# Attention before a routed expert layer: where the loads of q, k and v are asked for

## The chip, the cores and the metric

The kernel runs on one core of one Trainium2 chip. The metric is device time in microseconds (us) of one execution. The core has a matrix engine (PE, with its weight loads shown as PEld), a vector engine (DVE), a scalar engine (ACT), a general engine (POOL) and a sync engine (SP) that here does little but issue DMAs.

## The reference

Attention over 8 batches of 8 heads, 576 tokens of 64 channels, with a causal mask and a bias that decays with a running sum of `s`; then each token goes through one of eight two-layer experts, chosen by a gate that may keep the expert of the token before.

```python
scores = scale * np.matmul(q, k.transpose(0, 1, 3, 2))
bias = -(cum[:, :, :, None] - cum[:, :, None, :])
scores = np.where(causal, -1000000000.0, scores + np.minimum(bias, 0.0))
attn = np.exp(scores - np.max(scores, axis=-1, keepdims=True))
attn = attn / (np.sum(attn, axis=-1, keepdims=True) + 1e-09)
x = np.matmul(attn, v)            # heads side by side: 512 channels a token
...
h = np.maximum(x[b, s] @ w1[e], 0.0)
out[b, s] = p[e] * (h @ w2[e])
```

## The kernel before, in words

Two heads of a batch make one unit `n`; there are 32 of them (`NPAIR`). The attention part is a loop over 16 **slots** `m`; slot `m` works on the units `2m` and `2m+1`. All instructions are written in program order, one stream for each engine, and an engine takes its stream strictly in that order. In one slot PE does this:

1. **The stretch of scores** (`scores`, line 1125): six groups of matmuls, three for each of the two units, 40 matmuls in all. ACT takes the exponential of each group (line 1126), POOL masks it.
2. In some slots a router product (`lp`, line 230, in slots 4, 8, 12; `pos`, line 315, in slots 6, 10, 14).
3. **The stretch of values**: first the diagonal blocks of this slot's first unit (`values_halves`, line 1196), then the diagonal scores of the *next* slot's two units (`scores_halves(m + 1)`, line 1147, tile `ph`: 16 matmuls for unit `2m+2`, then 16 for unit `2m+3`), then line 1196 for the second unit, then 84 small matmuls into `po` and 84 into `pb` (`values`, line 1184). DVE divides and moves the results out (`evacuate`, line 1206), and later scales the v tiles of units to come (`weigh`, line 1102).

A unit needs three loads from DRAM: `kb` and `qb` (288 KB each, line 1273) and `va` (320 KB, line 1026). There are four buffers for `kb`, four for `qb` and six for `va`. The units 0 to 3 are loaded ahead of the loop; slot `m` asks for later units, six loads a slot, all on SP's queue. `transfers(m)` says at which place in the slot each load is asked for. A place is the end of one instruction: `e{u}{i}` is the exponential of group `u` of the slot's unit `i` (so `e00`, `e10`, `e20`, `e01`, `e11`, `e21` in the order of time, all belonging to the stretch of scores); `h` comes with the last exponential, but stands behind the diagonal scores in program order; `x0`, `x1` are the two reciprocals of the first unit's evacuation, `y0`, `y1` those of the second. SP waits for that instruction, then issues the DMA; SP's own stream is in program order too.

Other DMAs on SP in this part: `wx` (line 207, after slot 1's loads), `ends` and `wend` (lines 1090, 1092) and four stores of `table<-pad` (line 202) between the loads of slots 2 and 3; quarters of the first expert's weights (line 572) at `y1` of slots 11 to 14; fetches of rows from the table (line 582) in slot 14. POOL issues indirect stores into the table (line 363) in slots 6 to 15.

The scores of unit `n` are read in slot `n // 2`, but its diagonal scores one slot earlier:

```python
halves = banks("ph") if b + 1 < NPAIR else None
to = room(b)
scores_halves(m + 1, halves)
values_halves(b, to, True)
let_go("h", exps[b, 2])
```

Of the kernel before, what the change touches and what calls it, by code (L numbers as in the profile page):

```python
# [23 lines left out]
NPAIR = B * HP  # L24
# [97 lines left out]
def held(tc, dma, behind):  # L122

    if behind is not None:
        tc.add_manual_dep(dma.ins, behind.name, mybir.DependencyInfo(mybir.DependencyClass.Sync, mybir.DependencyReason.DATA),
                          reason="a transfer's time")
# [860 lines left out]
def attention(ctx, tc, q, k, v, s, wx, ident, recs, wend, router, experts):  # L987
# [32 lines left out]
    def load_v(n, behind=None):  # L1020

        if n >= NPAIR:
            return
        b, hp = divmod(n, HP)
        va = vs[n] = p_v.tile([P, NB, 2, DH], F32, name="va")
        held(tc, nc.sync.dma_start(va.rearrange("p c h d -> p (c h d)"), v[b, hp].rearrange("p c h d -> p (c h d)")), behind)
# [207 lines left out]
    for g in range(NG - 1):  # L1234
        m = HP * GB // 2 * (g + 1)
# [9 lines left out]
        for c in range(NC):  # L1245
# [3 lines left out]
            i, p = places[c]  # L1249
# [3 lines left out]
    m = NPAIR // 2  # L1253
# [14 lines left out]
    def qk_part(n, what):  # L1268
        def load(behind):
            b, hp = divmod(n, HP)  # L1270
            to = p_in.tile([P, S], F32, name=what + "b")
            ins.setdefault(n, [None, None])["qk".index(what)] = to
            held(tc, nc.sync.dma_start(to, (q, k)["qk".index(what)][b][:, hp]), behind)
        return load

    def v_part(n):
        return lambda behind: load_v(n, behind)

    def transfers(m):

        n = 2 * m + NV
        k0, q0, k1, q1 = (qk_part(n + i, x) for i in range(2) for x in "kq")
        if m == 0:
            return {"e11": v_part(4), "h": k0, "x0": q0, "x1": k1, "y0": q1}
        if m == 1:
            return {"e00": v_part(5), "e10": v_part(6), "e20": k0, "e11": q0, "h": k1, "x0": q1, "x1": v_part(7)}
        of = {"e00": v_part(n), "e20": v_part(n + 1), "e11": k0, "h": q0, "x0": k1, "x1": q1} if n < NPAIR else {}
        i = m - NPAIR // 2 + 5
        if 0 <= i < 4:
            of["y1"] = lambda behind: experts.load(0, 0, i, behind)  # L1290
        return of
# [7 lines left out]
    for m in range(NPAIR // 2):  # L1299
        pair = 2 * m, 2 * m + 1  # L1300
        waiting = transfers(m)
        for n in pair:
            for u in range(len(UNITS)):
# [623 lines left out]
```

## Time and profile before

| | |
|---|---|
| median of three runs | 695.86 us (693.32, 695.86, 697.61) |
| profiled execution, its own time | 695.28 us |
| its span, first to last instruction | 693.4 us |
| mean granted TensorE clock | 0.998 |
| PE busy | 674.5 us, 97% of the span |
| DVE, POOL, ACT busy | 525.5, 385.9, 199.9 us |
| moved by DMA | 158.18 MB, mean 228 GB/s |

The span runs from the first to the last instruction; the execution's own time has 1.88 us around it. The attention loop takes the first 205 us or so, the expert layer the rest. Times of rows are from the start of the span.

### The profile page before, as it was taken

The numbers are of one execution on the slowest core, as the hardware profiler recorded it, in microseconds if no ns is written. First come the engines' busy times: TensorE is split into PE (matmuls) and PEld (weight loads), VectorE is DVE, ScalarE is ACT, GpSimd is POOL, SyncE is SP. The second block draws the span as 40 slices with busy tenths as digits, with TensorE's granted clock in tenths as the row PEclk, the third lists the DMA queues.
The fourth block names the chain that finished last, engine by engine and source line by source line (L and its number), as shares of the span: only waits on it lengthen the run. The fifth ranks groups of instructions, "written<-read, shape, count | busy, mean of one in ns | idle before, by whom it ended". The sixth has DMA issues, their size and how long they took to land.

```text
span 693.4 us, 19173 instructions
## 1 busy us (share of the span) xinstructions
PE 674.5 (97%) x7837; PEld 586.2 (85%) x7837; DVE 525.5 (76%) x978; ACT 199.9 (29%) x368; POOL 385.9 (56%) x547
## 2 busy tenths in 40 slices
PE   8999989989999999999999999999999999999995
PEld 7787877878888889999998999999687997779984
DVE  4564857877975797989989997787568686779762
ACT  5454635536432112122221221212121122112121
POOL 3462366867776768746446367555433473525642
PEclk9999999999999999999999999999999999999999
DMA  8565565767659888499848447264988979866001
GB/s 259 186 207 157 158 199 154 229 202 229 204 158 406 254 274 300 152 335 350 302 187 302 156 169 287 88 257 140 349 289 336 394 282 317 270 251 257 31 13 39
DMA packets 54968, 158.18 MB, mean 228 GB/s; under 512 B 11156, under 2 KB 31636, under 8 KB 49111
## 3 DMA queue, kind: packets, MB, share of 16 engines
q1 hardware_dynamic: 47751, 136.52, 58.6%
q0 software_dynamic: 6880, 20.10, 7.6%
q8 instruction: 64, 1.05, 0.6%
q14 instruction: 33, 0.27, 0.1%
q10 hardware_dynamic: 240, 0.25, 0.1%
HBM read 136.21 MB, written 20.85 MB: 227 GB/s over the span
## 4 chain that ended last, share of the span: by engine, by line
PE 89%; DVE 3%; issue 3%; DMA 2%; POOL 1%; ACT 1%; POOLq 0%; ACTq 0%; DVEq 0%
PE p L687 27%; PE p L691 26%; PE ps L1125 11%; PE po L1184 6%; PE pb L1184 6%; PE hp L781 4%; PE hp L772 2%; PE yp L804 2%; DMA w1b<-in_w_dram 2%; PE lp L230 1%; PE ph L1147 1%; PE po L1196 1%; DVE wt L617 1%; DMA qb<-in_q_dram 1%; PE pb L1196 1%
## 5 line engine op out<-in xcount | busy, mean ns | idle before, releaser
L691 PE MATMUL p<-w2b,hT 128*128 128x256 f32 (+1 forms) x720 | 164.9, 380 | 1.9 <-DVE w2b L617 1.1
L691 PEld LDWEIGHTS p<-w2b,hT 128*128 128x128 f32 (+1 forms) x720 | 132.8, 187 | 24.6 <-issue 3.1
L687 PE MATMUL p<-xT,w1b 128*128 128x128 f32 (+1 forms) x1280 | 151.2, 275 | 1.4 <-DVE w1b L617 0.9
L687 PEld LDWEIGHTS p<-xT,w1b 128*128 128x128 f32 x1280 | 147.8, 192 | 4.4 <-issue 1.6
L1126 ACT ACTIVATE e<-ps 128x1024 f32<-128x1024 f32 (+2 forms) x96 | 79.9, 931 | 60.9 <-PE ps L1125 60.7
L756 POOL DMA_INDIRECT out_dram<-y,gi x38 | 45.0, 1185 | 82.0 <-ACT y L715 74.1
L715 ACT ACTIVATE y<-y,gi 128x256 f32<-128x256 f32 (+1 forms) x72 | 35.5, 506 | 166.3 <-DVE y L711 154.2
L716 ACT ACTIVATE hT<-hT 128x512 f32<-128x512 f32 (+1 forms) x64 | 39.0, 615 | 153.2 <-DVE hT L711 153.2
L1125 PE MATMUL ps<-qb,kb 64*128 64x64 f32 (+5 forms) x644 | 81.3, 403 | 0.7 <-DMA qb<-in_q_dram 0.4
L1125 PEld LDWEIGHTS ps<-qb,kb 64*128 64x128 f32 x644 | 53.0, 187 | 26.9 <-ACT e L1126 7.4
L668 POOL TENSOR_TENSOR hT<-hT,hS 128x512 f32<-128x512 f32 (+1 forms) x18 | 26.6, 1476 | 87.4 <-PE p L691 87.3
L691 PE MATMUL p<-wt,hS 128*128 128x256 f32 (+1 forms) x288 | 68.0, 379 | 0.0
L1109 POOL TENSOR_SCALAR_AFFINE_SELECT e<-e 128x128 f32<-128x128 f32 (+2 forms) x96 | 41.7, 448 | 43.4 <-ACT e L1126 42.8
L363 POOL DMA_INDIRECT table<-xb,idx x54 | 56.7, 1050 | 14.9 <-issue 12.6
L687 PE MATMUL p<-xS,wt 128*128 128x128 f32 (+1 forms) x512 | 62.4, 275 | 0.0
L691 PEld LDWEIGHTS p<-wt,hS 128*128 128x128 f32 (+1 forms) x288 | 53.8, 187 | 8.4
L687 PEld LDWEIGHTS p<-xS,wt 128*128 128x128 f32 x512 | 59.7, 192 | 0.0
L1184 PE MATMUL pb<-vg,e 128*64 128x66 f32 x1344 | 44.2, 223 | 5.0 <-issue 4.8
L1184 PEld LDWEIGHTS pb<-vg,e 128*64 128x64 f32 x1344 | 41.7, 138 | 6.2 <-issue 5.9
L1184 PE MATMUL po<-vg,e 128*64 128x66 f32 x1344 | 43.0, 223 | 0.6 <-issue 0.6
L1184 PEld LDWEIGHTS po<-vg,e 128*64 128x64 f32 x1344 | 40.6, 138 | 1.9 <-issue 0.8
L1102 DVE TENSOR_TENSOR vg<-va,wk 128x256 f32<-128x256 f32 x64 | 39.0, 674 | 0.0
(286 smaller groups left out, 960.3 us busy)
## 6 DMA issues: line engine op xcount, KB each, us to landing
w2b<-in_w_dram SPq DMA_DIRECT2D x23, 2048.0 KB, 12.4
w1b<-in_w_dram SPq DMA_DIRECT2D x22, 2048.0 KB, 12.9
va<-in_v_dram SPq DMA_DIRECT2D x32, 320.0 KB, 3.0
kb<-in_k_dram SPq DMA_DIRECT2D x31, 288.0 KB, 3.1
qb<-in_q_dram SPq DMA_DIRECT2D x31, 288.0 KB, 4.7
xq<-table SPq DMA_DIRECT2D x60, 130.0 KB, 3.1
w1b<-in_w_dram SPq DMA_DIRECT2D x4, 512.0 KB
xq<-table SPq DMA_DIRECT2D x12, 113.8 KB, 11.6
```

Of the source, the lines that this page charges most:

```text
L363: put = self.nc.gpsimd.indirect_dma_start(out=self.halves, in_=src, element_offset=0, in_offset=None, out_offset=bass.IndirectOffsetOnAxis ...
L687: mm(ps[:, m * h : m * h + h], lhsT=b[:, k, m * P : m * P + P], rhs=a[:, k, :], start=m == 0 and k == 0, stop=m == FK // 2 - 1 and k == n - 1)
L691: mm(ps[:h, : D // 2], lhsT=a[:, k, :], rhs=b[:, k, :], start=k == 0, stop=k == n - 1)
L715: return nc.scalar.mul(to, to, gi[:h, r, 1:2]).ins
L716: return nc.scalar.activation(to, to, Act.Relu).ins
L756: put = nc.gpsimd.indirect_dma_start(out=self.out[:, :], out_offset=bass.IndirectOffsetOnAxis(ap=gi.bitcast(I32)[:m, n, 0:1], axis=0), in_ ...
L781: mm(ps, lhsT=self.ws[ls[0]][0][:, k, c * P : c * P + P], rhs=xT[:, k, :w], start=(k == 0), stop=(k == DK - 1))
L1102: nc.vector.tensor_tensor(vg[:, to].rearrange("p c h e -> p (c h) e")[:, :, :DH], va[:, :c].rearrange("p c h e -> p (c h) e"), wk[:, n, to ...
L1109: nc.gpsimd.affine_select(out=ap, in_=ap, compare_op=Alu.is_ge, fill=0.0, base=base, pattern=n, channel_multiplier=-1)
L1125: mm(ps[:, h, at : at + z - a], lhsT=kb[d, key : key + P], rhs=qb[d, a:z], start=True, stop=True)
L1126: exps[n, u] = nc.scalar.activation(e[:, :, : WIDTH[u]], ps, Act.Exp, scale=scale).ins
L1184: of = mm(po[part][d, j - a, :], lhsT=weights_of(n, c, j, h), rhs=vgs[n % NV][:, c if j < 2 * G1 else G1 + c, h, :], start=(first and i == ...
```

## The change

`transfers` gives the six loads other places and another order. In slot `m` (from 2 on, `n = 2m + 4`) it was: v of `n` at `e00`, v of `n+1` at `e20`, k of `n` at `e11`, q of `n` at `h`, k of `n+1` at `x0`, q of `n+1` at `x1`. It is now: k and q of `n-1` at `e00` and `e10`, k and q of `n` at `e20` and `e01`, v of `n` and `n+1` at `e11` and `e21`. So the second unit of a slot's loads (k and q) is asked for one slot later than before, at the start of the next slot.

```diff
     def transfers(m):
         n = 2 * m + NV
-        k0, q0, k1, q1 = (qk_part(n + i, x) for i in range(2) for x in "kq")
+        ks, qs = ([qk_part(n + i, x) for i in (-1, 0)] for x in "kq")
         if m == 0:
-            return {"e11": v_part(4), "h": k0, "x0": q0, "x1": k1, "y0": q1}
-        if m == 1:
-            return {"e00": v_part(5), "e10": v_part(6), "e20": k0, "e11": q0, "h": k1, "x0": q1, "x1": v_part(7)}
-        of = {"e00": v_part(n), "e20": v_part(n + 1), "e11": k0, "h": q0, "x0": k1, "x1": q1} if n < NPAIR else {}
+            return {"e20": ks[1], "e01": qs[1], "e11": v_part(4), "e21": v_part(5)}
+        of = {"e00": ks[0], "e10": qs[0]} if n - 1 < NPAIR else {}
+        if n < NPAIR:
+            of |= {"e20": ks[1], "e01": qs[1], "e11": v_part(n), "e21": v_part(n + 1)}
         i = m - NPAIR // 2 + 5
         if 0 <= i < 4:
             of["y1"] = lambda behind: experts.load(0, 0, i, behind)
```

SP, the loads of slot 1 and what stands right behind them, as it was (`DMAHW` names one of eight semaphores that DMAs signal when they have landed; each issue waits for the DMA eight before it; `Activation`, `DVE`, `PE` and `Pool` stand for waits on those engines):

```order
L1026 DMA va_426<-in_v_dram 128x640 [waits DMAHW6_49,Activation_49]
L1026 DMA va_435<-in_v_dram 128x640 [waits DMAHW7_49,Activation_49]
L1273 DMA kb_444<-in_k_dram 128x576 [waits DMAHW0_49,Activation_49]
L1273 DMA qb_461<-in_q_dram 128x576 [waits DMAHW1_49,Activation_49]
L1273 DMA kb_510<-in_k_dram 128x576 [waits DMAHW2_49,Activation_49]
L1273 DMA qb_522<-in_q_dram 128x576 [waits DMAHW3_49,DVE_49]
L1026 DMA va_560<-in_v_dram 128x640 [waits DMAHW4_49,DVE_49]
L207 DMA wx_642<-in_wx_dram 128x256 [waits DMAHW5_49]
```

The same place now:

```order
L1273 DMA kb_424<-in_k_dram 128x576 [waits DMAHW5_49,Activation_49]
L1273 DMA qb_433<-in_q_dram 128x576 [waits DMAHW6_49,Activation_49]
L1273 DMA kb_442<-in_k_dram 128x576 [waits DMAHW7_49,Activation_49]
L1273 DMA qb_452<-in_q_dram 128x576 [waits DMAHW0_49,Activation_49]
L1026 DMA va_461<-in_v_dram 128x640 [waits DMAHW1_49,DVE_49,Activation_49]
L1026 DMA va_470<-in_v_dram 128x640 [waits DMAHW2_49,DVE_49,Activation_49]
L207 DMA wx_638<-in_wx_dram 128x256 [waits DMAHW3_49]
```

The k and q loads went ahead of the v loads; every load now waits for an exponential, and the v loads name DVE as well, for the buffer that they take over.

PE, in slot 1, from the diagonal blocks to the start of the values, as it was:

```order
L1147 MATMUL ph_480<-qb_355,kb_350 64x64 [waits DMAHW3_49,DMAHW2_49,Activation_49]
L1147 MATMUL ph_480<-qb_355,kb_350 64x64 x7
L1147 MATMUL ph_480<-qb_371,kb_359 64x64 [waits DMAHW5_49,DMAHW4_49]
L1147 MATMUL ph_480<-qb_371,kb_359 64x64 x7
L1196 MATMUL pb_481<-vg3_134,eh_322 64x66 [waits DVE_49,Activation_49]
```

And now:

```order
L1147 MATMUL ph_482<-qb_227,kb_217 64x64 [waits DMAHW2_49,DMAHW1_49,Activation_49]
L1147 MATMUL ph_482<-qb_227,kb_217 64x64 x7
L1147 MATMUL ph_482<-qb_433,kb_424 64x64 [waits DMAHW6_49,DMAHW5_49]
L1147 MATMUL ph_482<-qb_433,kb_424 64x64 x7
L1196 MATMUL pb_483<-vg3_134,eh_328 64x66 [waits DVE_49,Activation_49]
```

The order of PE's work is the same, but the third row read `qb_371` and `kb_359`, which slot 0 had asked for; it now reads `qb_433` and `kb_424`, the first two loads that slot 1 itself asks for (the first two rows of the fence before).

SP, from slot 2's last loads to slot 3's first, now (in the kernel before the same seven DMAs `ends`, `wend` and `table` stood there, with slot 2's last q ahead of them and slot 3's two v loads behind):

```order
L1026 DMA va_694<-in_v_dram 128x640 [waits DMAHW1_49,DVE_49,Activation_49]
L1090 DMA ends<-ends_783 64x9 [waits DMAHW2_49,Pool_49]
L1092 DMA wend_66<-ends 64x288 [waits DMAHW3_49,DMAHW2_49]
L1092 DMA wend_66<-ends 64x288 [waits DMAHW4_49]
L202 DMA table<-pad_878 128x260 [waits DMAHW5_49,Pool_49]
L202 DMA table<-pad_878 128x260 [waits DMAHW6_49]
L202 DMA table<-pad_878 128x260 [waits DMAHW7_49]
L202 DMA table<-pad_878 128x260 [waits DMAHW0_49]
L1273 DMA kb_895<-in_k_dram 128x576 [waits DMAHW1_49,Activation_49]
L1273 DMA qb_904<-in_q_dram 128x576 [waits Activation_49]
```

What moved is which load comes first behind those seven: it is now a pair of k and q that slot 3's own diagonal scores read.

## The prediction, as it was put on record

> **What bounds the kernel now.** I read the page first, its busy times and the chain that ended last.
>
> ```profile
> PE 674.5 (97%) x7837; PEld 586.2 (85%) x7837; DVE 525.5 (76%) x978; ACT 199.9 (29%) x368; POOL 385.9 (56%) x547
> PE 89%; DVE 3%; issue 3%; DMA 2%; POOL 1%; ACT 1%; POOLq 0%; ACTq 0%; DVEq 0%
> ```
>
> PE is the bound, and DMA has 2% of the chain. A change of loads can win only PE's idle time and can lose whatever makes PE wait. So the second view is the chain in order of time, over one slot (start, length, what). Slot 1:
>
> ```profile
> 19.52 4.96 PE ps L1125 x40
> 24.48 0.39 PE po L1196 x16
> 24.87 0.47 PE ph L1147 x32
> 25.57 2.60 PE po L1184 x84
> 28.18 2.33 PE pb L1184 x80
> 30.51 0.72 issue
> 31.57 4.96 PE ps L1125 x40
> ```
>
> Scores take 4.96 us, then values follow with hardly a hole, but for 0.72 us of "issue" near the end. The third view, the list of waits cut to PE and the attention loop, has two rows that sum those holes:
>
> ```profile
> PE pb L1184 <- issue: 4.8, 5, 1.7
> PE po L1184 <- issue: 0.6, 1, 0.6
> ```
>
> That is 5.4 us in six holes, all in values; one (0.6 us, in `po`) is in slot 15, which asks for no q, k or v. At most 4.8 us is there to be won.
>
> What are the holes? I looked at busy times by stretch (length, PE busy, PEld, DVE, ACT, POOL, clock, DMA share, GB/s), one row for the values of slots 1, 5, 7 and 14:
>
> ```profile
> 24.41:31.50 7.09, 6.37 (x235) 6.14 (x233) 1.89 (x6) 1.92 (x5) 4.66 (x20) 1.00 0.83 263
> 73.06:79.21 6.15, 6.15 (x235) 6.01 (x233) 5.58 (x21) 2.14 (x6) 2.23 (x5) 1.00 0.56 159
> 96.31:104.46 8.15, 6.41 (x234) 6.13 (x232) 1.88 (x6) 2.14 (x6) 6.19 (x12) 1.00 0.82 252
> 184.51:191.37 6.86, 6.86 (x239) 6.57 (x237) 6.11 (x20) 1.94 (x4) 3.08 (x8) 1.00 0.47 111
> ```
>
> Where the DMA engines are busy 0.82 or 0.83 of the stretch, PE loses 0.72 and 1.74 us; at 0.56 and 0.47 it loses nothing. The DMA queues over 28.90 to 28.95 us show what starts there, 1.6 us ahead of slot 1's hole: a packet of the instruction queue (packets, MB, share).
>
> ```profile
> q8 instruction: 1, 0.02, 118.4%
> ```
>
> My reading: values run through instructions faster than scores, and the fetch of PE's next block comes late when loads crowd the DMA engines. Against this stands the Trainium skill, page "Runtime: NRT & Kernel Launch", section "Instruction fetch mechanics": crossing a 16 KiB boundary is one DMA tail-bump, "mostly hidden". By that rule nothing is to be won in the holes, and the sum below would be 1.0 us higher; the six holes, up to 1.7 us, speak for a fetch that is not always hidden.
>
> **The change, part by part.** It adds and removes no instruction. It moves six loads a slot.
>
> *The pair that becomes urgent.* k and q of unit 2m+3, asked for in slot m-1 before, are now asked for in slot m at `e00` and `e10`, and the second half of the same slot's `ph` reads them. Slot 1 of the kernel before happens to use the same two places, for v; SP's rows:
>
> ```profile
> 21.74 0.33 SPq L1026 DMA_DIRECT2D va<-in_v_dram  x1
> 22.54 0.94 SPq L1026 DMA_DIRECT2D va<-in_v_dram  x1
> ```
>
> So k goes out 21.74 - 19.52 = 2.22 us after the scores begin, q at 3.02 us. PE reaches `ph` at 24.87 - 19.52 = 5.35 us and its second half 0.23 us later, at 5.58 us. The q must land within **2.56 us** of its issue, or PE stands still. Landings, from the rows of single issues (a q with no load just ahead; then a q 0.75 us behind its k; then the page's median of all q):
>
> ```profile
> L1273 SPq DMA_DIRECT2D qb<-in_q_dram x1: 328/328/328, 66.0 to 66.0; - x1
> DMA to landing us min/median/max: 2.7/2.7/2.7
> 178.37 0.33 SPq L1273 DMA_DIRECT2D kb<-in_k_dram  x1
> 179.12 0.33 SPq L1273 DMA_DIRECT2D qb<-in_q_dram  x1
> DMA to landing us min/median/max: 3.9/3.9/3.9
> qb<-in_q_dram SPq DMA_DIRECT2D x31, 288.0 KB, 4.7
> ```
>
> Even the lone one is too late by 0.14 us. The new q stands 0.8 us behind a k, like the one that took 3.9 us, but with fewer transfers in flight in the early slots. I take 3.4 us in slots 1, 2 and 5, between 2.7 and 3.9 and nearer the second: a wait of 3.4 - 2.56 = 0.85 us. POOL's table stores run in slots 6 to 15, and the v of slot 10 shows their weight, 4.4 us:
>
> ```profile
> L1026 SPq DMA_DIRECT2D va<-in_v_dram x1: 328/328/328, 133.3 to 133.3; - x1
> DMA to landing us min/median/max: 4.4/4.4/4.4
> ```
>
> For slots 7, 9, 11 and 13 I take 3.9 us: 1.3 us each. In slots 6, 10 and 14 `pos` holds PE back, and in slots 4, 8 and 12 `lp`:
>
> ```profile
> 59.72 2.31 PE lp L230 x64
> 79.28 4.96 PE ps L1125 x40
> 84.24 0.46 PE pos L315 x2
> 85.34 0.47 PE ph L1147 x32
> ```
>
> With `lp`, `ph` comes 2.31 us later and no wait is left. With `pos` it comes at 85.34 - 79.28 = 6.06 us, 0.71 us later: 0.15 us in slot 6, 0.6 us in 10 and 14. Sum without slot 3: 3 x 0.85 + 4 x 1.3 + 0.15 + 2 x 0.6 = 9.1 us. By the ends 2.7 and 4.7 us: seven full slots at 0.14 or 2.14 us give 1 to 15 us, and the three with `pos` add 0 to 4 us.
>
> The Trainium skill, page "DMA: Bandwidth & Descriptors", section "Anatomy of one DMA — SWDGE (gpsimd) path", fits a transfer by about 2.0 us plus its bytes over 436 GB/s, for another issuing path. By it, as an estimate, the pair lands 3.35 us after k is issued, 2.55 us after q, and this whole sum is nil. The pair at 178.37 took 0.75 + 3.9 = 4.65 us, so I go by the row.
>
> *Slot 3.* Seven DMAs stand on SP ahead of the urgent pair:
>
> ```profile
> 39.58 0.31 POOL L1088 COPY ends<-xb 64x4 f32<-64x4 f32 x2
> 40.94 0.71 SPq L1090 DMA_DIRECT2D ends<-ends  x1
> 43.76 1.11 SPq L1092 DMA_DIRECT2D wend<-ends  x2
> 44.96 2.02 SPq L202 DMA_DIRECT2D table<-pad  x4
> 47.08 1.08 SPq L1026 DMA_DIRECT2D va<-in_v_dram  x2
> 42.67 4.96 PE ps L1125 x40
> L1273 SPq DMA_DIRECT2D qb<-in_q_dram x1: 328/328/328, 49.1 to 49.1; - x1
> DMA to landing us min/median/max: 5.7/5.7/5.7
> ```
>
> `ends` now waits for POOL's copies, not for slot 2's last q, and goes out some 0.2 us earlier; slot 3 starts 0.85 us later. So the first load behind the pads, at 47.08 - 42.67 = 4.41 us of the slot, comes at about 3.35 us, q 0.45 us behind it at 3.8. A q of this slot took 5.7 us; with the best at 3.9 I take 4.6: landing at 8.4 us, a wait of 2.8 us (2.1 to 5.0).
>
> *Behind the wait.* PE holds back its line 1196, `po` and `pb`, and DVE's evacuations behind them; ACT's exponential of `ph` and POOL's mask of it feed the next slot, a whole slot away. SP waits for exponentials, which lie ahead of the wait. So only PE's time grows, by the wait itself. Slot 15 has no `ph`, and behind it the chain runs on PE into the experts, so the loss reaches the end whole.
>
> *The loads taken out of values.* Asked for by the end of scores is not landed by then: v at `e21` is issued some 6 us into the slot. Of 1.8 MB a slot, asked for from 2.2 us on, at the 250 GB/s of full stretches above, about 0.7 MB moves within scores and the rest in the first half of values, where the fetch of the block for `pb` must pass. q of the second unit no longer spills into the next scores. So the holes can vanish (-4.8 us) or come in each of the 14 slots at slot 1's price (14 x 0.72 - 4.8 = +5.3). I take -1.0, since PE's wait lets the loads drain first.
>
> *What costs nothing.* v comes up to 4 us later in its slot; `weigh`, its first reader, stands behind the slot's last evacuation, at 11 us or later, and v asked at 6 lands by 10.4 at 4.4 us. Were that cover gone, DVE would wait, a slot ahead of PE's need. `wx` moves up with no wait. The expert's weight quarters at `y1` keep their place ahead of a slot's first load; in slot 14 the pair goes ahead of the table fetches, which wait for stores anyway. At most eight DMAs may be open; six a slot stay under it. Scores take 4.96 us in every slot, whether loads run beside them or not, so more of them there cost nothing.
>
> **Sum**, against the profiled execution's 695.28 us (span 693.4 and 1.88 around it, 0.6 below the median): 9.1 + 2.8 - 1.0 = +10.9, so **706 us**.
>
> **Rivals.**
>
> - *The pair lands in time.* At 2.7 us the wait is 0.14 in seven slots and 0.9 in slot 3 (3.8 + 2.7 - 5.58): +1.9 - 1.0, 696 us. For it: nothing else is in flight at 2.2 us of a quiet slot. Against: no load here landed under 2.7 us, and q shares the engines with k. The skill's fit above is this case. Chance 0.17.
> - *Faster: the fetch gets through.* The holes are an instruction fetch behind loads; if the new loads are done before each fetch, all 4.8 us go. With the pair at 2.7 us: 695.3 + 1.9 - 4.8 = 692.4 us. It decides if waits average under 0.3 us a slot. Against: the rest of six loads moves exactly where the fetch runs. Chance 0.08.
> - *Both get worse.* Six loads crowded together delay every slot's fetch as in slot 1: +5.3 in place of -1.0, 712 us. Slot 1 of before, with loads at the same places, has its hole. Chance 0.13.
> - *The loads are not out of values.* That is in my sum: they are asked for earlier but still move there.
>
> **How the numbers follow.** My forecast has 0.62, with its own range 700 to 713. The range, 696 to 715, adds the upper case and the case of a pair in time; outside stay the faster case and the long end. A measurement tells about 1%, 7 us: under 689 only by more than the known holes (0.04); within, the first two rivals and the low end of mine (0.27); slower the rest (0.69).
>
> **What would show it.** In the waits of after, PE `ph` L1147 held by a DMA of `qb` or `kb`, about ten times, 9 us or so, the longest in slot 3; no such wait in slots 4, 8 and 12. "issue" ahead of `pb` at 2 to 6 us. Expert stretches as long as before. I am wrong if `ph` starts at 5.4 us in slots 1, 2 and 5, or if PE's holes vanish.

## The result: slower, by twice what was forecast

| | before | after |
|---|---|---|
| median of six runs | 695.66 us (692.59 to 697.61) | 718.12 us (715.25 to 722.22) |
| ratio after to before, 95% interval | | 1.0336 (1.0290 to 1.0382) |
| profiled execution, its own time | 695.28 us | 716.72 us |
| its span | 693.4 us | 714.8 us |

The forecast was 706 us with a range of 696 to 715. The direction held and the size did not: +21.4 us between the two profiled executions, where the sum said +10.9.

The page of after: busy times, and the shares of the chain that ended last.

```profile
PE 680.0 (95%) x7837; PEld 590.7 (83%) x7837; DVE 523.0 (73%) x978; ACT 200.7 (28%) x368; POOL 386.3 (54%) x547
PE 76%; DMA 9%; DVE 5%; issue 4%; ACT 3%; POOL 1%; SPq 0%; POOLq 0%; DVEq 0%; ACTq 0%
```

DMA went from 2% to 9% of the chain. PE is also 5.5 us *busier* with the same 7837 matmuls, so waits alone cannot be the whole story. PE's waits in the attention loop (us in total, times, the longest):

```profile
PE ph L1147 <- DMA qb<-in_q_dram: 14.4, 10, 2.5
PE pb L1184 <- issue: 6.1, 5, 1.9
PE po L1184 <- issue: 0.4, 1, 0.4
PE ph L1147 <- issue: 0.4, 1, 0.4
```

The first row is the wait that the forecast named, ten times as it said, but 14.4 us long in place of 11.9. The holes in `pb`, which were to shrink, grew. The chain in order of time (start, length, what), the rows of slot 1 from its first scores on (the load of q counted from its issue):

```profile
19.58 1.08 PE ps L1125 x4
...
22.60 3.98 DMA qb<-in_q_dram
...
26.71 0.46 PE ph L1147 x16
...
27.41 2.60 PE po L1184 x84
```

Scores begin at 19.58. Without a wait the second half of `ph` would start 5.58 us later (the prediction's figure), at 25.16; it starts at 26.71. The difference, 1.55 us, is the wait. The same rows of slots 3, 7, 9 and 13 (where each slot's q is asked for, and where PE starts again):

```profile
45.53 1.08 PE ps L1125 x4
...
48.86 4.17 DMA qb<-in_q_dram
...
53.17 0.71 PE ph L1147 x16
...
54.32 3.63 PE po L1184 x84
...
99.99 1.08 PE ps L1125 x4
...
103.02 3.46 DMA qb<-in_q_dram
...
106.62 0.46 PE ph L1147 x16
...
128.11 1.08 PE ps L1125 x4
...
131.13 4.97 DMA qb<-in_q_dram
...
136.24 0.46 PE ph L1147 x16
...
188.31 4.69 DMA qb<-in_q_dram
...
194.19 3.67 PE po L1184 x84
```

By the same reading the waits are 2.06 us in slot 3, 1.05 in slot 7, 2.55 in slot 9. Two things here were in no term of the sum. In slots 3 and 13 the 84 matmuls of `po` take 3.63 and 3.67 us, where they take 2.60 us in slot 1. And behind *every* wait the 16 matmuls of `ph` take at least 0.46 us, where the kernel before did all 32 in 0.47. Slot 6, for which the profile counts no wait, has the 0.46 us as well.

Busy times by stretch (length, PE busy, PEld, DVE, ACT, POOL, granted clock, DMA share, GB/s): the values of slots 1, 3 and 9, then a stretch of 3.41 us in slot 3 and one in slot 13:

```profile
24.47:32.39 7.92, 6.37 (x234) 6.13 (x233) 1.89 (x6) 2.04 (x5) 4.54 (x20) 1.00 0.61 208
50.42:60.33 9.91, 7.85 (x235) 7.55 (x233) 3.92 (x9) 2.32 (x4) 2.91 (x5) 0.83 0.50 179
133.00:142.45 9.45, 6.64 (x235) 6.25 (x233) 5.88 (x21) 2.25 (x6) 6.15 (x12) 1.00 0.64 212
53.07:56.48 3.41, 3.31 (x72) 3.21 (x74) 0.63 (x2) 0.60 (x1) 1.31 (x2) 0.50 0.68 256
193.02:196.43 3.41, 3.38 (x74) 3.26 (x76) 1.62 (x6) 0.80 (x3) 2.50 (x5) 0.50 0.93 358
```

Right behind the waits of slots 3 and 13 the granted clock was **0.50** for one stretch of 3.41 us. The values of slot 3 then keep PE busy for 7.85 us rather than 6.37, and those of slot 13 for 7.89: 3.0 us in the two slots. Slot 9 waited longest of all and kept its clock at 1.00.

**Where the 21.4 us lie.** Slot 1 starts at 19.45 in the trace of before and at 19.51 in that of after; slot 15 starts at 191.37 and at 212.92. Slots 1 to 14 thus grew by 21.5 us, and what follows them not at all. Made up of:

| | forecast | measured |
|---|---|---|
| waits for the pair in slots 1, 2, 5 | 2.55 | 1.55 + 1.74 + 1.54 = 4.8 |
| in slots 7, 11 | 2.6 | 1.05 + 1.12 = 2.2 |
| in slots 9, 13 | 2.6 | 2.55 + 2.17 = 4.7 |
| in slots 6, 10, 14 | 1.35 | 0 + 0.24 + 0.41 = 0.65 |
| in slot 3 | 2.8 | 2.06 |
| holes in `po` and `pb`, slots 1 to 14 | −1.0 | 6.1 + 0.4 − 4.8 = 1.7 |
| half clock in slots 3 and 13 | not seen | 3.0 |
| slow start of `ph` in eleven slots, 0.23 each | not seen | 2.5 |
| sum | 10.9 | 21.6 |

The sum is within 0.2 us of the measured growth. (The stop of 0.4 us ahead of `ph` in the list above is in slot 0, ahead of this stretch.) This much is bookkeeping; why each term has its size is the matter of the experiments.

### The profile page after: what moved, and what is told of

It reads as the page before. It is cut to its first block, busy times and chain, and to the rows that moved or that the text cites. A ratio compares the mean times of both kernels' runs of the same rounds, so it can differ in the third digit from the quotient of the medians.

```text
span 714.8 us, 19173 instructions
## 1 busy us (share of the span) xinstructions
PE 680.0 (95%) x7837; PEld 590.7 (83%) x7837; DVE 523.0 (73%) x978; ACT 200.7 (28%) x368; POOL 386.3 (54%) x547
## 3 DMA queue, kind: packets, MB, share of 16 engines
q8 instruction: 64, 1.05, 0.6%
## 4 chain that ended last, share of the span: by engine, by line
PE 76%; DMA 9%; DVE 5%; issue 4%; ACT 3%; POOL 1%; SPq 0%; POOLq 0%; DVEq 0%; ACTq 0%
PE p L691 27%; PE p L687 23%; PE po L1184 6%; DMA qb<-in_q_dram 6%; PE pb L1184 5%; PE ps L1125 5%; PE hp L781 4%; DMA w1b<-in_w_dram 3%; ACT e L1126 2%; PE hp L772 2%; DMA w2b<-in_w_dram 1%; PE ph L1147 1%; DVE wt L617 1%; PE lp L230 1%; PE yp L804 1%
## 5 line engine op out<-in xcount | busy, mean ns | idle before, releaser
L1184 PE MATMUL po<-vg,e 128*64 128x66 f32 x1344 | 45.6, 229 | 0.5 <-issue 0.4
L1184 PEld LDWEIGHTS po<-vg,e 128*64 128x64 f32 x1344 | 43.0, 143 | 2.2 <-issue 0.9
```

What stands on the lines that cost most here:

```text
L1184: of = mm(po[part][d, j - a, :], lhsT=weights_of(n, c, j, h), rhs=vgs[n % NV][:, c if j < 2 * G1 else G1 + c, h, :], start=(first and i == ...
```

## The experiments

Two of the three sets of runs fell on chips on which the kernel before itself takes 717 us, so each run below is compared, by its ratio, with runs of the kernel before on the same chip. The first two entries show what such a chip does to both kernels.

### Both kernels again, on a chip where before takes 717 us

No edit.

> The kernel before, for a trace on the same chip as the runs beside it. Either theory: no wait of PE at ph for q or k; holes ahead of po and pb only.

> The changed kernel, for a trace on the same chip as the runs beside it. Theory: 2 to 4% over the kernel before, PE's waits at ph 10 to 16 us, and a half-clock row wherever PE idles some 1.9 us or more inside one stretch of 3.4 us.

Before: 717.21 us in its profiled run, after: a ratio of 1.0246 (1.0192 to 1.0300). PE's waits in before, then in after:

```profile
PE pb L1184 <- issue: 6.5, 16, 1.2
PE po L1184 <- issue: 2.1, 7, 0.4
```

```profile
PE ph L1147 <- DMA qb<-in_q_dram: 12.7, 10, 2.3
PE pb L1184 <- issue: 10.5, 14, 1.7
```

The change brings the same things here as there, for a smaller share of the time: ten waits for a q, and half-clock stretches (at 52.84 and 199.62 us, and at 247.4 us behind the loop). What differs is the background, in both kernels: many more short "issue" stops, 23 of them in `pb` and `po` of before where the first trace had six. Why these chips have them was not found out.

### Which part of the change costs: the pair put back, and the pair alone

The edits are cut to the lines for slots from 2 on; `ks[2]` and `qs[2]` are the loads of unit `n+1`.

```diff
 e1_pair_back, against after
-        of = {"e00": ks[0], "e10": qs[0]} if n - 1 < NPAIR else {}
+        of = {}
         if n < NPAIR:
-            of |= {"e20": ks[1], "e01": qs[1], "e11": v_part(n), "e21": v_part(n + 1)}
+            of |= {"e20": ks[1], "e01": qs[1], "e11": v_part(n), "e21": v_part(n + 1), "x0": ks[2], "x1": qs[2]}

 e2_pair_alone, against before
-        of = {"e00": v_part(n), "e20": v_part(n + 1), "e11": k0, "h": q0, "x0": k1, "x1": q1} if n < NPAIR else {}
+        of = {"e00": ks[0], "e10": qs[0]} if n - 1 < NPAIR else {}
+        if n < NPAIR:
+            of |= {"e20": v_part(n), "e01": v_part(n + 1), "e11": ks[1], "h": qs[1]}
```

> Only the pair is undone: k and q of unit 2m+5 are asked for at x0 and x1 of slot m again, the other four loads stay where the change put them. Theory (PE waits at ph for a pair that is asked for in the same slot: 14.4 us of waits, 3.0 us of matmuls at half the clock behind the two longest, some 2 us of slower restarts): all of that goes, the holes in the values stay at 5 to 8 us, total 694 to 700 us. Rival (crowding loads into the stretch of scores is what costs): it stays above 710 us.

> Only the pair is moved: k and q of unit 2m+3 at e00 and e10 of slot m, then v, v, k, q at e20, e01, e11, h. Theory: PE waits at ph in the slots without lp, 12 to 15 us in all, total 708 to 717 us. Rival (crowding): about 696 us, since the other loads stand nearly as before.

With the pair back, the four other loads at their new places: ratio 1.0027 (1.0004 to 1.0050). With the pair alone moved: 1.0234 (1.0202 to 1.0267), which covers after's 1.0246 on such a chip. The longest row of PE's waits in the first, and in the second:

```profile
PE pb L1184 <- issue: 8.1, 17, 1.3
```

```profile
PE ph L1147 <- DMA qb<-in_q_dram: 12.5, 10, 2.5
```

The moved pair is the loss, but for some 0.3%. Without it there is no wait for a q and no half clock in the loop; with it alone, two half-clock stretches in the loop and one behind it (at 27.19, 201.27 and 249.06 us). The absolute times of the expectation missed by the chip's 21 us. The four other loads, moved out of values, gained nothing: the holes in `pb` are 8.1 us, against 6.5 in before on a like chip.

### Is the half clock a loss of its own: PE kept busy through the wait

The added matmuls alone are shown:

```diff
 e3_filled, ahead of the second half of ph in slots 3 and 13
+            if i and m - 1 in (3, 13):
+                for _ in range(6):
+                    mm(whole[:, 0, 4 * DH : 4 * DH + P], lhsT=ident, rhs=ident, start=True, stop=True)

 e9_filled_all, in eight slots
+            if i and m - 1 in (1, 2, 3, 5, 7, 9, 11, 13):
+                for _ in range(3):
+                    mm(whole[:, 0, 256:512], lhsT=ident, rhs=wk.rearrange("p n c h -> p (n c h)")[:, :256], start=True, stop=True)
```

> The changed kernel with six extra 128x128 matmuls (results unused) ahead of the second half of ph in slots 3 and 13 alone, the two slots whose values ran at half the granted clock; they run inside PE's wait of 2.1 us there. Theory (the clock is halved because PE idles too long inside one fixed stretch of 3.4 us): no half-clock row within the attention loop, 84 matmuls of po back from 3.63 to 2.60 us in both slots, total 3 us less than the changed kernel (715 against 718). Rival (those slots are slow for what DMA does there): both stay at 3.6 us and 718 us.

> The changed kernel with three extra matmuls of 256 columns (1.1 us, results unused) ahead of the second half of ph in slots 1, 2, 3, 5, 7, 9, 11 and 13: they run inside PE's wait. Theory (PE idle in one stretch of 3.4 us halves the clock in the next): no half-clock row in the attention loop, waits at ph shorter by what the fillers take, total 0 to 4 us less than the changed kernel, by 1.5 us for each half-clock row that it has. Rival (the half clock has another cause): the rows stay, total the same or longer by the fillers.

Ratios 1.0259 (1.0207 to 1.0312) and 1.0249 (1.0227 to 1.0271): no lower than after on such chips. Each of these calls makes two matmuls on PE (the pages count 24 and 48 more than for after), so the fillers take 1.60 and 1.56 us a slot, not the 1.1 us expected of the second. The clock did what was expected in the two slots. Slot 3 of `e9_filled_all`, by stretch (slot 13 has 1.00 as well):

```profile
51.50:62.00 10.50, 9.21 (x232) 8.05 (x232) 5.77 (x12) 4.01 (x6) 4.32 (x8) 1.00 0.61 202
```

But half-clock stretches came up elsewhere, in `e9_filled_all` at 18.36 and 117.35 us, in `e3_filled` at 18.23, 117.22 and 178.66. The second of `e3_filled`, and the stop that the chain of that run shows ahead of it:

```profile
117.22:120.63 3.41, 3.41 (x45) 2.77 (x43) 1.20 (x3) 0.22 (x1) 0.36 (x2) 0.50 0.10 32
```

```profile
114.12 2.15 issue
```

Ahead of the other two stand stops of 2.02 us (at 16.17, in slot 0's `ph`) and 2.30 us (at 174.97, in `pb`). None of the three is a wait for a load. So the half clock comes after stops of other causes too, and can be taken away from a slot. That the kernel gets faster by it was not shown. The "issue" stops ahead of `ph`, `po` and `pb` sum to 16.8 us in `e3_filled` and 13.4 in `e9_filled_all`, against 12.1 in `a2_after`; why the added instructions made them larger was not told apart. And in slots 1, 7, 9 and 11, where `a2_after` waits 0.74 to 1.22 us, a filler of 1.56 us is longer than the wait, by about 2.4 us in all.

### Why q lands late in slots 1, 2, 5 and 9: the instruction stream shifted

In after, one packet of the instruction queue starts 2.41, 1.97, 2.12 and 2.68 us into slots 1, 2, 5 and 9, and is still on its way when q goes out at 3.09 us; in slots 7, 10, 11, 13 and 14 none is near. The queue's row of slot 5 there (packets, MB, share of the engines):

```profile
q8 instruction: 1, 0.02, 3.7%
```

q lands 3.97 to 4.97 us after its issue in slots 1, 2, 5 and 9, and 3.38 to 3.56 in slots 7, 10, 11 and 14. Slot 13 does not fit: it has no packet and 4.69 us. A 512 KB load of expert weights goes out 1.9 us ahead of its k; whether that is the reason was not tested. The theory: a 16 KB fetch of PE's instructions stands beside the pair on a DMA engine and delays it. The rival: those slots are late for other reasons. Forty tiny matmul calls in the warm-up move all of PE's instructions behind them. The expectation counts 80 instructions for them. Each call makes two matmuls on PE, with a weight load each (the page has PE x7917, after x7837), so the move was one of 160:

```diff
 e5_shift_80, in the warm-up, against after
+        for i in range(40):
+            mm(warm[:32, :1], lhsT=zero[:, :32], rhs=zero[:, :1], start=True, stop=True)
```

> The changed kernel with 40 tiny extra matmuls (results unused) in the warm-up, so that all later PE instructions stand 80 places further on in their 256-instruction blocks. In the changed kernel an instruction packet is fetched about 2 to 3.6 us into slots 1, 2, 5 and 9, beside the urgent pair; counted out, with 80 places more none falls there in any slot from 1 to 14. Theory (the 16 KB instruction packet holds up one DMA engine, and the pair lands with its last engine): in slots 1, 2 and 5 the second half of ph starts 3.3 to 3.8 us after q's issue instead of 3.8 to 4.8, so PE's waits there are 0.7 to 1.2 us each. Rival (those early slots are slow for another reason): they stay at 3.8 us and more. The total says little, since the holes in the values move as well: 1 to 4% over the kernel before.

Ratio 1.0406 (1.0365 to 1.0448), on a chip where before takes 695.64 us: at the upper end of the expected 1 to 4%. Lines stand two further down here. Slots 1, 2, 5 and 7 in the chain, and PE's longest row of waits:

```profile
26.12 3.35 DMA qb<-in_q_dram
...
38.38 3.26 DMA qb<-in_q_dram
...
80.82 3.35 DMA qb<-in_q_dram
...
107.00 4.95 DMA qb<-in_q_dram
```

```profile
PE ph L1149 <- DMA qb<-in_q_dram: 17.8, 11, 3.0
```

Slots 1, 2 and 5, now without a fetch beside the pair, land in 3.35, 3.26 and 3.35 us, and their waits fall from 1.55, 1.74 and 1.54 to 0.92, 0.83 and 0.93 us: the expected 0.7 to 1.2, and near the 0.85 that the prediction had put there. Slots 7 and 10, which have got a fetch, go from 3.46 to 4.95 and from 3.38 to 5.50 us. The fetches were expected to fall into none of the waiting slots; with twice the move they fell into slots 3, 6, 7, 9, 10, 11 and 13, and the waits of these slots made up the total. In slots 3 and 11 q was not late (3.60 and 3.38 us): there the packet had ended 0.4 and 0.3 us before q went out. In slots 1, 2, 5, 7 and 10 the delay went with the fetch, in both directions.

### The q asked for earlier

```diff
 e8_both_e00, against after
-        of = {"e00": ks[0], "e10": qs[0]} if n - 1 < NPAIR else {}
+        of = {"e00": lambda behind: (ks[0](behind), qs[0](behind))} if n - 1 < NPAIR else {}
```

> The changed kernel with q of the urgent pair asked for at e00 together with its k, 0.4 instead of 0.8 us behind it. Theory (PE's wait is the landing of q minus 2.56 us): ph starts 0.3 to 0.5 us earlier in each of the eleven slots without lp, total 3 to 6 us less than the changed kernel. Rival (the pair is held up by the amount in flight, not by when it is asked for): no change.

Ratio 1.0283 (1.0263 to 1.0303): no gain, where 3 to 6 us were expected. q went out some 0.4 us earlier and landed 3.1 to 5.0 us after its issue.

```profile
PE ph L1147 <- DMA qb<-in_q_dram: 12.9, 9, 2.9
```

Over the loop, an earlier issue did not make an earlier landing. Slot by slot it went both ways: slot 2, which lost its fetch in this run, waited 0.28 us (1.53 in `a2_after`), slot 11 waited 2.15 (0.98). A pair's landing is not issue plus a constant here; the fetches are one part of it, and the rest was not settled.

### k and q asked for a slot ahead, and the holes

The lines taken out are left out:

```diff
 e4_ask_late, against after
+        of = {}
+        if n < NPAIR:
+            first = ("e11", "e21") if m == 0 else ("e00", "e10")
+            of = {first[0]: v_part(n), first[1]: v_part(n + 1), "x1": both(ks[1], qs[1]), "y0": both(ks[2], qs[2])}

 e10_late_early_pads, in addition
+            if m == 2:
+                of["x0"], of["x1"] = of["x1"], of.pop("y0")
```

(`both` issues its two loads at one place.) The four k and q go out late in values, 9.0 to 10.4 us into slot 1 of 11.1 us, for the diagonal scores of the next slot, so that they move beside scores; only v is asked for within scores.

> All six loads moved out of the time in which PE's instructions for the values are fetched: v and v at e00 and e10, then k and q of 2m+4 at x1 and k and q of 2m+5 at y0, a slot ahead of their use. Theory (the holes in the values, 5.4 us before, are an instruction fetch behind load packets): holes fall to 1 to 3 us, no wait at ph, 691 to 694 us. Rival (the holes do not depend on the loads): holes of 5 us, 695 to 697 us.

> All six loads asked for outside the time of PE's instruction fetch (v and v at e00 and e10, the k and q pairs at x1 and y0 a slot ahead), and in slot 2 at x0 and x1, ahead of ends, wend and the table stores on SP's queue. Without the last, slot 3 had a wait of 3.0 us at ph and a slot of 17.1 us instead of 12.6. Theory: slot 3 falls to 11 to 12 us, no wait at ph anywhere, total 0.1 to 0.6% under the kernel before. Rival (the loads behind x1 and y0 cost elsewhere what they save): the same or slower.

The first missed its expectation: ratio 1.0046 (1.0025 to 1.0067), a wait of 3.0 us at `ph`, and 6.7 us of stops in `po` and `pb`, where before on a like chip has 8.6. Its one wait for a q is in slot 3, and the chain shows why: a `y0` pair of slot 2 stood on SP behind `ends`.

```profile
41.58 4.32 DMA ends<-ends
...
47.70 3.57 DMA qb<-in_q_dram
```

That stop was 3.0 us and was followed by half clock for 6.83 us; slot 3 took 17.1 us, where slots 1 and 2 took 11.1. With slot 2's pairs put ahead of `ends`, on the faster chip: **692.58 us against 695.64, ratio 0.9964 (0.9944 to 0.9983)**, the one version that beats both kernels, and by what was expected; two waits of up to 0.3 us at `ph` were not. Its waits, and slot 1 in its chain:

```profile
PE po L1184 <- issue: 0.9, 1, 0.9
PE ph L1147 <- DMA qb<-in_q_dram: 0.5, 2, 0.3
PE pb L1184 <- issue: 0.3, 1, 0.3
```

```profile
25.40 0.47 PE ph L1147 x32
...
26.10 2.60 PE po L1184 x84
28.70 2.45 PE pb L1184 x84
```

And the stretch of values of that slot:

```profile
24.20:31.00 6.80, 6.80 (x242) 6.56 (x240) 2.01 (x7) 2.66 (x6) 4.62 (x20) 1.00 0.33 97
```

`ph` runs its 32 matmuls in one go, the hole of slot 1 (0.72 us before) is gone, and the DMA share of its values is 0.33, where the prediction showed 0.83. The holes fell from 5.4 to 1.2 us with PE's instructions in the same order, and slot 15 starts at 187.18 rather than 191.37.

That shows that the loads make the holes. That they do it by way of the instruction fetch is shown by where PE stops. Slot 7 in before, in after and in `e5_shift_80`:

```profile
100.07 0.93 PE pb L1184 x30
101.00 1.74 issue
```

```profile
109.91 0.93 PE pb L1184 x30
110.84 1.79 issue
```

```profile
115.39 2.33 PE pb L1186 x78
117.71 0.34 issue
```

Before and after stop ahead of the same matmul, though their loads stand elsewhere. Counted along PE's matmuls, the "issue" stops of before and after in `ph`, `po` and `pb` are ahead of numbers 218, 599, 1106, 1996, 2249, 2885, 3139, 3392, 3645 and 4536: the distances are multiples of 127, to within 2. Each matmul has one weight load, so 127 of them are 254 instructions. In `e5_shift_80` all work stands 80 matmuls further on, and the stops are ahead of 346, 1488, 1743, 2377, 2631, 3520 and 3773: the same grid, and so other work. The instruction queue moved 64 packets in all of before; PE's 15,674 matmuls and weight loads make 62 stretches of 254. So the holes stand at fixed places of the instruction stream, and loads in flight there open them. (On the slower chip most of the extra stops lie off this grid, in groups 0.7 to 0.8 us apart: they are something else.)

The Trainium skill, page "Runtime: NRT & Kernel Launch", section "Instruction fetch mechanics", has that cost mostly hidden; here 4.2 us of stops went when the loads were moved, and 3.1 us of a 696 us kernel with them.

## Why the prediction failed, point by point

- **What bounds the kernel**: right. PE is the bound, the pair is nearly the whole loss (`e1_pair_back`, `e2_pair_alone`), and it reaches the end whole.
- **The pair that becomes urgent**: the mechanism, the waiting slots (but for slot 6, where 0.15 us was forecast and none showed) and the free slots 4, 8 and 12 were right. The term was mis-sized: 9.1 us forecast, 12.35 measured (14.4 less slot 3). It failed at "I take 3.4 us in slots 1, 2 and 5", which took 3.97 to 4.16: without a fetch it is 3.3 to 3.5 us (slots 7 and 11, and `e5_shift_80`), but a fetch lies beside the pair in just these slots and in 9. The 3.9 us for slots 7, 9, 11 and 13, put down to POOL's stores, sorted them wrongly: two took 3.5, two 4.7 and 5.0. The prediction had found such a fetch behind slot 1's *hole* and did not ask which load stands beside it.
- **Slot 3**: 2.8 forecast, 2.06 measured, just under its low bound of 2.1: q went out 3.3 us into the slot, not 3.8, and landed in 4.17 us, not 4.6.
- **The holes**: −1.0 forecast, +1.7 measured; "PE's wait lets the loads drain first" failed. The cause named for them held (`e10_late_early_pads` and the places of the stops); what failed is that asking in scores takes loads out of values, which the prediction itself had doubted. Slots 1 and 3 did lose their holes; slots 6, 10, 11 and 12 lost 0.4 to 0.9 us more each. Why those and not the others was not tested.
- **Behind the wait**: "only PE's time grows, by the wait itself" is the step that failed. A stop also costs a slow start, 0.23 us, and in two slots half a clock: 5.5 us together, which is the growth of PE's busy time. It is the largest of the misses. The slow start could have been read off before: the prediction's own rows have PE busy for 6.37 us in slot 1, which has a hole, and 6.15 us in slot 5, which has none. The half clock could not: no hole of before was followed by one.
- **The range**: it took the unknown landing from 2.7 to 4.7 us slot by slot and left out that a stop may slow what follows it. The two terms not seen, 5.5 us, would by themselves have put the forecast near 712.

The Trainium skill, page "TensorE: Matmul & The Clock Gate", Part 1 ("The HAM clock gate"), gives the gate a free-running window of 3413 ns and lets the clock fall after an idle one. The traces agree on the length and on the free run. They differ on the idle time: about 2 us within one window was enough, as told below.

## What to carry to other kernels

A load moved later is priced by its landing beside everything that moves at that place, instruction fetches too, and against the time at which its reader is there; when that margin is a few tenths of a microsecond, the move is a loss waiting for a place. A stop of a matmul engine costs more than its length: add the slow start, and if it nears 2 us (1.6 us was the least here), the chance of a stretch at half clock. To keep loads away from a stretch that suffers from them, ask for them a whole stretch ahead, not at its start, and look at what else stands in the queue in front of them.

## What the hardware showed that was not expected

- **Half clock after 2 us of idle.** In after, PE stopped from 51.11 to 53.17, and clock 0.50 came from 53.07 to 56.48; of the 3.41 us before that, 1.96 were idle. In slot 13 it was 2.14 us. The three stretches of `e3_filled` followed holes with 2.0 to 2.2 us in the 3.41 us before. Slot 9's stop of 2.55 us, laid on the same grid of 3.413 us, falls 1.29 us into one window and 1.26 into the next: no half clock. So the share of a fixed window counts, and not the length of a stop alone. Over all twelve traces, each laid on the grid of its own half-clock stretches, every window with 1.96 us of idle or more was followed by half clock and none with less than 1.64 behind the warm-up, but for one: in `e4_ask_late` the half clock lasted a second window, though only 0.73 us of the first were idle. Between 1.64 and 1.93 both came: after was idle for 1.87 us from 152.06 to 155.47 and kept its clock, `e8_both_e00` for 1.64 from 197.66 to 201.07 and lost it. What else decides there stays open.
- **A 16 KB instruction packet delays a 288 KB load** by 0.6 to 2.1 us when it is still on its way as the load goes out (slots 1, 2, 5, 7 and 10 of after and `e5_shift_80`, each with and without one). In the two slots in which it had ended by then, the load took 3.38 and 3.60 us.
- **PE stops for instructions at fixed places** of its stream, 127 matmuls apart or a multiple of it, when loads are in flight there: up to 1.87 us in after, and 1.2 us in all in `e10_late_early_pads`.
- **Chips differ by 3%** for the same kernel (695.6 and 717 us), with more short stops of PE on the slower ones.
